# Loading SSM constants as rows, transposing them on TensorE, and moving the first exponentials behind a square root

## The chip, the cores and the metric

One core of a Trainium2 chip runs the whole kernel. The metric is the device time of one execution in microseconds (us), and lower is better. A timed run gives six or so executions; I quote their median and range. A profile is taken of one execution, and its "span" runs from the first to the last instruction; the device time is some 1.8 us longer than the span.

The engines: TensorE (PE) multiplies, VectorE (DVE) and ScalarE (ACT) work on elements, GpSimd (POOL) and SyncE (SP) mostly issue transfers. PSUM is the memory that PE writes; here it is cut into four slots.

## The reference, cut to what matters

```python
xn = layernorm(x)                                    # S=2048 rows, D=576 columns
# state space model with 576 states
dt = exp(log_dt);  Lam_bar = exp(dt * (Lambda_re + 1j*Lambda_im))
B_bar = ((Lam_bar - 1) / Lam)[:, None] * (B_re + 1j*B_im)
h[t] = Lam_bar * h[t-1] + xn[t] @ B_bar.T
ssm = 2 * real(h @ C.T) + xn * Dskip
# gated feed-forward, F=4608
ffn = (sigmoid(xn @ w_gate) * (xn @ w_up)) @ w_down
out = x + ssm + ffn
```

The three vectors `log_dt`, `Lambda_re`, `Lambda_im` have 576 values each. They are needed as per-partition columns: one state per partition, five columns.

## The kernel before

PE does nearly everything that counts: gate/up "groups" of 18 matmuls (two 64-row halves side by side, tile `pgu`), down-projection steps (`pd`), and the SSM's input projections (`pbu`). ACT evacuates each gate/up group from PSUM (sigmoid into `sT`, copy into `uT`), and DVE multiplies the two into `hT`. All other work of DVE and ACT (layernorm of later blocks, residuals, exponentials, angle tables) waits in a background queue. Each evacuation grants it some credit, and it then puts tasks into the instruction streams, in the order in which they were added:

```python
class Background:
    def gap(self): ...            # rest until the next step
    def step(self, us):           # called after each evacuation
        self.now += 1
        self.credit = min(self.credit + us, 5.0)
        while True:
            q = self.head()       # first task whose `ready` holds
            if q is None or q[0][0] > self.credit: return
            cost, fn, _ = q.popleft(); self.credit -= cost; fn()
```

Each engine runs its own stream in order, so a task that is put ahead of an evacuation delays it. The constants are loaded late, one value per partition, by nine POOL-issued transfers, and the exponentials follow much later:

```python
def load_consts():                                    # called after the first 8 groups
    for (dst, src) in ((ldt, A_log_dt), (lre, A_Lambda_re), (lim, A_Lambda_im)):
        nc.gpsimd.dma_start(dst[:, 0:PT], src[0:R0].rearrange("(a p) -> p a", p=P))
        for h0 in (0, H):
            nc.gpsimd.dma_start(dst[h0:h0 + H, PT:NU], src[R0:NS].rearrange("(a b) -> a b", b=1))

def exp_first():
    nc.scalar.activation(dt[:], ldt[:], ACT.Exp)
    nc.vector.tensor_mul(r5[:], dt[:], lre[:])
    nc.scalar.activation(r5[:], r5[:], ACT.Exp)
```

The start, where four PSUM slots hold two gate/up groups and two transpose tiles:

```python
start_groups = [GateUp(0, f, 0) for f in range(2)]
ptrs = [psum.tile([P, NH, P], BF16, name="ptr", tag="ps") for _ in range(2)]
...                                   # block 0: layernorm, PE transposes, first halves
for tt in range(2, TT_B):
    start_copy(tt, slice(0, 5), nc.scalar.copy)
    start_copy(tt, slice(5, NH), nc.vector.tensor_copy)
for g in start_groups:
    g.mms(slice(2 * P, TB))           # second halves of groups 0 and 1
for tt in range(TT_B, 2 * TT_B):
    bg.add(1.05, lambda tt=tt: ln_stats(tt))          # DVE, block 1
bg.gap()
bg.add(0.0, lambda: ln_std(1, 0, TT_B))               # ACT square root
bg.add(0.2, lambda: ln_recip(1, 0, TT_B))
...                                   # normalise, transpose, residuals
bg.gap()
bg.add(1.0, exp_first, ready=...)
bg.gap()
bg.add(1.5, angles_small)             # then ten angle tables on DVE
bg.step(3.2)
for g in start_groups:
    g.evac(); used(g); bg.step(4.5)
```

## Time and profile before

| | us |
|---|---|
| device time, median of 3 | 510.02 (508.99 to 510.29) |
| with three more, median of 6 | 509.67 (508.61 to 510.29) |
| profiled execution: device time, span | 508.32, 506.5 |
| PE busy | 500.9, 99% of the span |

Two rows from the page's costliest groups (line, engine, operation, output and inputs, shapes, count; then busy us and mean ns of one; then the engine's idle time just before them and who ended most of it):

```profile
L495 PE MATMUL pgu<-xT,wgu 64*128 64x512 bf16 (+1 forms) x2628 | 283.7, 373 | 0.0
L569 PE MATMUL pd<-wd,hT 128*128 128x288 bf16 x1152 | 144.8, 286 | 0.4 <-DVE hT L504 0.4
```

The two kinds of matmul wait for others for 0.4 us in all. So in this execution almost nothing can be won by making another engine faster.

### The profile page before, as it was taken

To read this page: it belongs to the slowest core of one execution; us is meant where nothing else is said; L and a number is where in the kernel's file an instruction comes from. 1 tells how busy PE (TensorE), PEld (TensorE's weight loads), DVE (VectorE), ACT (ScalarE), POOL (GpSimd) and SP (SyncE) were. 2 spreads that over 40 slices of the span, in tenths; PEclk is the share of its full clock that TensorE was granted. 3 is DMA by queue.
4 is the path that set the end of the run, shared out by engine and by line. 5 is a ranking of instruction groups with operands and counts; after the bars stand their busy time and mean duration, and the time that the engine had idled before them with its cause. 6 is when DMAs were issued, how large, how long until landed. Compare 5 with 4: busy or idle time off the path is not lost.

```text
span 506.5 us, 10662 instructions
## 1 busy us (share of the span) xinstructions
PE 500.9 (99%) x4536; PEld 290.1 (57%) x4536; DVE 324.1 (64%) x703; ACT 204.9 (40%) x368; POOL 96.9 (19%) x143
## 2 busy tenths in 40 slices
PE   8999999999999999999999999999999999999997
PEld 6444575444477444477754444774444774446775
DVE  6964999886888797868878767786765222221111
ACT  4767623556500756520035655006555005553000
POOL 7138420123100043110001231000431001300000
PEclk9999999999999999999999999999999999999999
DMA  8999895246220099261430652200753201600001
GB/s 211 206 181 163 204 188 98 55 110 141 49 48 25 1 145 199 58 149 37 89 77 11 155 132 55 49 25 1 160 114 79 48 25 39 171 1 4 33 25 36
DMA packets 42959, 45.59 MB, mean 90 GB/s; under 512 B 30496, under 2 KB 34336, under 8 KB 42912
## 3 DMA queue, kind: packets, MB, share of 16 engines
q0 software_dynamic: 12672, 34.23, 31.1%
q1 hardware_dynamic: 29808, 10.33, 10.7%
q8 instruction: 35, 0.57, 0.5%
q10 hardware_dynamic: 432, 0.37, 0.2%
q14 instruction: 12, 0.10, 0.1%
HBM read 34.36 MB, written 2.36 MB: 72 GB/s over the span
## 4 chain that ended last, share of the span: by engine, by line
PE 94%; DVE 3%; ACT 1%; DMA 1%; issue 0%
PE pgu L495 52%; PE pd L569 34%; PE pbu L524 7%; DVE sctab L325 1%; DVE rnd L324 1%; DMA xt<-in_A_x_dram 1%; DVE ang L349 1%; PE ptr L741 0%; DVE hT L504 0%; ACT xT L744 0%; DVE bnst L224 0%; ACT L328 0%; ACT uT L502 0%; ACT L501 0%; ACT sT L501 0%
## 5 line engine op out<-in xcount | busy, mean ns | idle before, releaser
L495 PE MATMUL pgu<-xT,wgu 64*128 64x512 bf16 (+1 forms) x2628 | 283.7, 373 | 0.0
L495 PEld LDWEIGHTS <-wgu 64*128 64x128 bf16 x2628 | 127.6, 94 | 151.1 <-issue 0.5
L569 PE MATMUL pd<-wd,hT 128*128 128x288 bf16 x1152 | 144.8, 286 | 0.4 <-DVE hT L504 0.4
L501 ACT ACTIVATE sT<-pgu 128x512 bf16<-128x512 f32 x144 | 86.4, 600 | 120.4 <-PE pgu L495 110.3
L569 PEld LDWEIGHTS <-hT 128*128 128x128 bf16 x1152 | 112.1, 98 | 31.3 <-DVE hT L504 1.5
L504 DVE TENSOR_TENSOR hT<-sT,uT 128x512 bf16<-128x512 bf16 x144 | 60.7, 423 | 100.3 <-ACT uT L502 100.1
L502 ACT CAST uT<-pgu 128x512 bf16<-128x512 f32 x144 | 83.9, 583 | 0.0
L154 POOL DMA_DIRECT2D wgu<-in_B_w_gate_dram x36 | 27.9, 776 | 227.2 <-PE pgu L495 208.2
L160 POOL DMA_DIRECT2D wd<-in_B_w_down_dram x36 | 26.6, 755 | 100.2 <-PE pd L569 100.2
L530 ACT COPY bure<-pbu 128x512 f32<-128x512 f32 x16 | 9.4, 588 | 87.8 <-PE pbu L524 75.4
L589 DVE TENSOR_TENSOR acc<-acc,pd 128x576 f32<-128x576 f32 x32 | 24.1, 752 | 24.5 <-PE pd L569 24.5
L586 DVE TENSOR_TENSOR ob<-acc,pd 128x576 bf16<-128x576 f32 x15 | 11.3, 754 | 38.0 <-PE pd L569 38.0
L524 PE MATMUL pbu<-xT,bt 64*128 64x512 bf16 x288 | 33.7, 376 | 0.0
L569 PEld LDWEIGHTS <-hst 128*128 128x128 bf16 x288 | 28.2, 98 | 7.1
L154 POOL DMA_DIRECT2D wgu<-in_B_w_up_dram x36 | 26.8, 745 | 2.7 <-DMA wgu<-in_B_w_up_dram 1.9
L569 PE MATMUL pd<-ctre,hst 128*128 128x288 bf16 x128 | 26.5, 286 | 0.0
L569 PE MATMUL pd<-ctim,hst 128*128 128x288 bf16 x128 | 26.5, 286 | 0.0
L439 DVE TENSOR_TENSOR_SCAN gre<-r,g0re,wrim 128x512 bf16<-128x512 f32 x20 | 25.6, 1279 | 0.0
L524 PEld LDWEIGHTS <-bt 64*128 64x128 bf16 x288 | 13.7, 94 | 17.1 <-issue 0.7
L446 DVE TENSOR_TENSOR_SCAN gim<-r,g0im,wrim 128x512 bf16<-128x512 f32 x16 | 20.4, 1275 | 0.0
L224 DVE BATCH_NORM_STATS2 bnst<-xt 128x6 f32<-128x288 bf16 x32 | 12.6, 435 | 2.2 <-DMA xt<-in_A_x_dram 2.2
L501 ACT ACT_TABLE_LOAD x6 | 7.7, 1283 | 15.5 <-PE pgu L495 15.4
(113 smaller groups left out, 280.8 us busy)
## 6 DMA issues: line engine op xcount, KB each, us to landing
wgu<-in_B_w_gate_dram POOLq DMA_DIRECT2D x36, 288.0 KB, 4.4
wgu<-in_B_w_up_dram POOLq DMA_DIRECT2D x36, 288.0 KB, 5.2
wd<-in_B_w_down_dram POOLq DMA_DIRECT2D x36, 288.0 KB, 6.1
out_dram<-ob SPq DMA_DIRECT2D x15, 144.0 KB, 1.8
xt<-in_A_x_dram SPq DMA_DIRECT2D x10, 144.0 KB, 2.8
xt<-in_A_x_dram POOLq DMA_DIRECT2D x4, 144.0 KB, 6.6
bt<-ctre POOLq DMA_DIRECT2D x2, 288.0 KB, 7.2
bt<-ctim POOLq DMA_DIRECT2D x2, 288.0 KB, 8.0
```

Source lines behind the costliest of these rows:

```text
L154: eng.dma_start(w[rows, :, :], src[:, fs].rearrange("(c p) f -> p c f", p=H))
L160: nc.gpsimd.dma_start(wd[:], B_w_down[f0:f0 + FP * P, :].rearrange("(n p) d -> p n d", p=P))
L224: nc.vector.bn_stats(st[:, gi, :], xt[:, gi * DH:(gi + 1) * DH])
L439: nc.vector.tensor_tensor_scan(gre[:], r_bc, w[:, 0, :], g0re[:, col], ALU.mult, ALU.add)
L446: nc.vector.tensor_tensor_scan(gim[:], r_bc, w[:, 1, :], g0im[:, col], ALU.mult, ALU.add)
L495: nc.tensor.matmul(self.ps[:, gi, cols], w[rows, c, fs], xT[self.nb][rows, c, cols], start=c == 0, stop=c == NH - 1)
L501: nc.scalar.activation(sT[:], self.ps[:, 0, :], ACT.Sigmoid)
L502: nc.scalar.copy(uT[:], self.ps[:, 1, :])
L504: nc.vector.tensor_mul(h[:], sT[:], uT[:])
L524: nc.tensor.matmul(out, w, xT[self.nb][rows, c, ts_], start=c == 0, stop=c == NH - 1)
L569: nc.tensor.matmul(out, lhsT, rhs[:, a * DH:(a + 1) * DH], start=i == 0, stop=i == n - 1)
L589: nc.vector.tensor_add(halves(acc[:]), halves(acc[:]), pd[:, :, 0:DH])
```

## The change

Its intent is to get the constants to the chip cheaply and early: three row loads of 64 states per partition instead of nine loads of single values, two small PE transposes in a spot where PE has its operands anyway, and the exponentials next to a square root, so that the long angle tables can start earlier. Apart from that, the last down-projection step is cut 448 + 128 columns rather than 288 + 288, so that less is left to do after the last matmul.

```diff
-    def load_consts(): ...                     # nine POOL loads, see above
+    cvals = consts.tile([P, 3, NU], FP32, name="cvals")
+    ldt, lre, lim = (cvals[:, i, :] for i in range(3))
+    crows = consts.tile([3 * NH, H], BF16, name="crows")
+    for i, src in enumerate((A_log_dt, A_Lambda_re, A_Lambda_im)):
+        nc.sync.dma_start(crows[i * NH:(i + 1) * NH, :], src.rearrange("(a p) -> a p", p=H))
+
+    def consts_transpose(ps):
+        for half in (slice(0, H), slice(H, P)):
+            nc.tensor.transpose(ps[half, 0:3 * NH], crows[:], ident[0:3 * NH, 0:3 * NH])
+
+    def consts_copy(ps):
+        rows = ps[:, 0:3 * NH].rearrange("p (i a) -> p i a", a=NH)
+        nc.vector.tensor_copy(cvals[0:H, :, :], rows[0:H, :, 0:NH:2])
+        nc.vector.tensor_copy(cvals[H:P, :, 0:PT], rows[H:P, :, 1:NH:2])
+        nc.vector.tensor_copy(cvals[H:P, :, PT:NU], rows[H:P, :, NH - 1:NH])
...
     def exp_first():
-        nc.scalar.activation(dt[:], ldt[:], ACT.Exp)
-        nc.vector.tensor_mul(r5[:], dt[:], lre[:])
-        nc.scalar.activation(r5[:], r5[:], ACT.Exp)
+        nc.scalar.activation(dt[:], ldt, ACT.Exp)
+        for a in range(NU):
+            nc.scalar.activation(r5[:, a:a + 1], lre[:, a:a + 1], ACT.Exp, scale=dt[:, a:a + 1])
...                                             # last step of the down projection
-            for a, eng in ((0, nc.sync), (1, nc.scalar)):
-                cs = slice(a * DH, (a + 1) * DH)
+            for eng, cs in ((nc.sync, slice(0, D - P)), (nc.scalar, slice(D - P, D))):
...
-    ptrs = [psum.tile([P, NH, P], BF16, name="ptr", tag="ps") for _ in range(2)]
+    ptrs = [psum.tile([P, NH + 1, P], BF16, name="ptr", tag="ps") for _ in range(2)]
...
-    for g in start_groups:
-        g.mms(slice(2 * P, TB))
+    start_groups[0].mms(slice(2 * P, TB))
+    consts_transpose(ptrs[1][:, NH, :])
+    consts_copy(ptrs[1][:, NH, :])
+    start_groups[1].mms(slice(2 * P, TB))
     for tt in range(TT_B, 2 * TT_B):
         bg.add(1.05, lambda tt=tt: ln_stats(tt))
     bg.gap()
     bg.add(0.0, lambda: ln_std(1, 0, TT_B))
+    bg.add(0.0, exp_first)
...
-    bg.gap()
-    bg.add(1.0, exp_first, ready=lambda: consts_at[0] is not None and consts_at[0] + 4 <= bg.now)
...
-                side_loads.extend([load_consts] + bt_loads)
+                side_loads.extend(bt_loads)
```

The cuts hide renamed operands (`lre[:]` to `lre` and the like), a loop of two loads written out, and the lines of the last step that follow from its new cut.

More of the change, by code (lines that the diff above doesn't have):

```diff
@@ L166 @@
         load_x(tt, nc.sync if tt % 2 == 0 else nc.scalar)
-    for pr in range(2):
-        load_wgu((0, pr), nc.gpsimd, nc.gpsimd)
+    load_wgu((0, 0), nc.gpsimd, nc.gpsimd)
+    load_wgu((0, 1), nc.gpsimd, nc.gpsimd)
     for tt in range(TT_B, 2 * TT_B):
@@ L184 @@
     xn_bufs = [consts.tile([P, NH, 2, H], BF16, name=f"xn{i}") for i in range(XN_BUFS)]
-    lre = consts.tile([P, NU], FP32, name="lre")
-    lim = consts.tile([P, NU], FP32, name="lim")
-    ldt = consts.tile([P, NU], FP32, name="ldt")
-    consts_at = [None]
-    def load_consts():
-        for (dst, src) in ((ldt, A_log_dt), (lre, A_Lambda_re), (lim, A_Lambda_im)):
-            nc.gpsimd.dma_start(dst[:, 0:PT], src[0:R0].rearrange("(a p) -> p a", p=P))
-            for h0 in (0, H):
-                nc.gpsimd.dma_start(dst[h0:h0 + H, PT:NU], src[R0:NS].rearrange("(a b) -> a b", b=1))
-        consts_at[0] = bg.now
+    cvals = consts.tile([P, 3, NU], FP32, name="cvals")
[11 more added lines that the diff above has]
+        nc.vector.tensor_copy(cvals[H:P, :, PT:NU], rows[H:P, :, NH - 1:NH])
     iota = ssmp.tile([P, TB], FP32, name="iota", tag="buim", bufs=2)
@@ L327, in exp_first @@
     def exp_first():
-        nc.scalar.activation(dt[:], ldt[:], ACT.Exp)
-        nc.vector.tensor_mul(r5[:], dt[:], lre[:])
-        nc.scalar.activation(r5[:], r5[:], ACT.Exp)
+        nc.scalar.activation(dt[:], ldt, ACT.Exp)
+        for a in range(NU):
+            nc.scalar.activation(r5[:, a:a + 1], lre[:, a:a + 1], ACT.Exp, scale=dt[:, a:a + 1])
     def angles_small():
-        nc.vector.tensor_mul(thc[:], dt[:], lim[:])
+        nc.vector.tensor_mul(thc[:], dt[:], lim)
         nc.vector.tensor_scalar_mul(thc[:], thc[:], 1.0 / TWO_PI)
@@ L365, in per_state_q @@
         nc.vector.tensor_mul(ni[:], r5[:], sn)
-        nc.vector.tensor_mul(m1[:], lre[:], lre[:])
-        nc.vector.tensor_mul(m2[:], lim[:], lim[:])
+        nc.vector.tensor_mul(m1[:], lre, lre)
+        nc.vector.tensor_mul(m2[:], lim, lim)
         nc.vector.tensor_add(m1[:], m1[:], m2[:])
         nc.vector.reciprocal(m1[:], m1[:])
-        nc.vector.tensor_mul(qre[:], nr[:], lre[:])
-        nc.vector.tensor_mul(m2[:], ni[:], lim[:])
+        nc.vector.tensor_mul(qre[:], nr[:], lre)
+        nc.vector.tensor_mul(m2[:], ni[:], lim)
         nc.vector.tensor_add(qre[:], qre[:], m2[:])
         nc.vector.tensor_mul(qre[:], qre[:], m1[:])
-        nc.vector.tensor_mul(qim[:], ni[:], lre[:])
-        nc.vector.tensor_mul(m2[:], nr[:], lim[:])
+        nc.vector.tensor_mul(qim[:], ni[:], lre)
+        nc.vector.tensor_mul(m2[:], nr[:], lim)
         nc.vector.tensor_sub(qim[:], qim[:], m2[:])
@@ L572, in d_step @@
             ob = lnp.tile([P, D], BF16, name="ob", bufs=2)
-            for a, eng in ((0, nc.sync), (1, nc.scalar)):
-                cs = slice(a * DH, (a + 1) * DH)
-                pd = ps_pair("pd")
+            for eng, cs in ((nc.sync, slice(0, D - P)), (nc.scalar, slice(D - P, D))):
+                pd = ps_pair("pd")[:, 0, 0:cs.stop - cs.start]
                 for i in range(n):
-                    mm(pd[:, 0, 0:DH], i, a)
-                nc.vector.tensor_add(ob[:, cs], acc[:, cs], pd[:, 0, 0:DH])
+                    lhsT, rhs = terms[i]
+                    nc.tensor.matmul(pd, lhsT, rhs[:, cs], start=i == 0, stop=i == n - 1)
+                nc.vector.tensor_add(ob[:, cs], acc[:, cs], pd)
                 eng.dma_start(o[tt * P:(tt + 1) * P, cs], ob[:, cs])
```

## The prediction

> **What bounds the kernel now.** I first read the page's busy times and its chain that ended last.
>
> ```profile
> PE 500.9 (99%) x4536; PEld 290.1 (57%) x4536; DVE 324.1 (64%) x703; ACT 204.9 (40%) x368; POOL 96.9 (19%) x143
> ...
> PE 94%; DVE 3%; ACT 1%; DMA 1%; issue 0%
> ```
>
> The columns are busy us, share of the 506.5 us span and instructions; the second line is the chain's share by engine. TensorE (PE) is the bound. But a busy PE can hide short waits, so I computed the distance from each matmul's start to the next over the whole trace. From 8.48 us (first real matmul) to 502.5 us the spacing is regular: 18 gate/up matmuls, two row halves running side by side, every 1.94 us; 123 ns between the 288-column matmuls of the down projection. Only one spacing stands out: 640 ns instead of 123, in the first down-projection step. The PE timeline shows where:
>
> ```profile
> 37.82 18.73 PE L495 MATMUL pgu<-xT,wgu 64*128 64x512 bf16 x172
> 56.48 2.87 PE L569 MATMUL pd<-wd,hT 128*128 128x288 bf16 x22
> 59.70 6.54 PE L569 MATMUL pd<-wd,hT 128*128 128x288 bf16 x52 [0.35 <-DVE hT L504]
> ```
>
> Columns: start us, duration us, engine, line, operation, tiles, count, and in brackets the idle time before and who ended it. After 22 matmuls (11 of 12 terms) PE waits for the twelfth hT, which VectorE (DVE) made late because it works on the angle tables in between. That wait costs 0.64 - 0.12 = 0.52 us. So the existing kernel has 0.52 us of PE wait to win between start and end, plus whatever lies before 8.48 us and after 502.79 us. Nothing else that gets faster on DVE, ScalarE (ACT), GpSimd (POOL) or a queue can shorten it. The reverse question is where PE has little slack. The timeline of the start answers it:
>
> ```profile
> 11.62 0.42 DVE L744 COPY xT<-ptr 128x512 bf16<-128x512 bf16 x1 [0.17 <-ACT xT L744]
> ...
> 11.96 0.81 DVE L224 BATCH_NORM_STATS2 bnst<-xt 128x6 f32<-128x288 bf16 x2
> ...
> 13.39 0.58 ACT L502 CAST uT<-pgu 128x512 bf16<-128x512 f32 x1
> ...
> 13.99 1.28 ACT L228 ACT_TABLE_LOAD   x1
> ...
> 16.16 0.30 ACT L228 ACTIVATE rstd<-mv,eps_t 128x4 f32<-128x4 f32 x1 [0.89 <-DVE mv L225]
> 16.48 1.28 ACT L501 ACT_TABLE_LOAD   x1
> ...
> 17.77 0.60 ACT L501 ACTIVATE sT<-pgu 128x512 bf16<-128x512 f32 x1
> 18.26 0.58 ACT L502 CAST uT<-pgu 128x512 bf16<-128x512 f32 x1
> ```
>
> ACT evacuates gate/up group 0 (until 13.97), then loads the square-root table and stands waiting for block 1's statistics until 16.16, reloads the sigmoid table and only then evacuates group 1 (done at 18.84). PSUM has four slots: two for the transposes, two for groups 0 and 1. Groups 2 and 3 take the transpose slots, group 4 that of group 0, group 5 that of group 1. The matmul starts in the trace put group 2 at 13.65 and group 5 at 13.65 + 3 x 1.94 = 19.48 us. So the slack of PE against group 1's evacuation is 19.48 - 18.84 = 0.64 us. This is the place to watch.
>
> **What the Trainium skill says.** "ScalarE: Activation LUTs", section What ACT_TABLE_LOAD costs: a table load measures about 1283 ns plus a drain of about 1380 ns. The trace agrees on the load (1283 ns in its groups) but not on a further drain: the load at 16.48 ends at 17.76 and the sigmoid starts at 17.77. I use 1.28. The same section says that each per-partition pointer operand adds about 93 ns to an ACTIVATE and that back-to-back ones overlap by about 93 ns; here a square root with a pointer bias takes 298 ns, the exponential without one 209, and the two square roots at 8.31 us take 0.49 together, so it agrees. "TensorEngine Tiling (Array Packing)", section Key Properties: changing the tiling mode drains the engine; here the step from the last transpose to the next gate/up matmul is 152 ns, against 28 between transposes. "TensorE: Matmul & The Clock Gate", section on the HAM clock gate: after one idle window of about 3.4 us the clock drops to half. This trace shows the clock at 1.0 throughout and no such gap after the start, so it cannot say; it matters below.
>
> **The change part by part.**
>
> *Loads.* Nine POOL-issued loads are removed (about 5.5 us of POOL issue from 35.02 to 40.5 us) and three on the SyncE queue behind x are added; that queue is idle until 17.60. POOL's weight loads move up, but PE waits for none of them: worth 0.
>
> *Two small transposes on PE* between the second halves of groups 0 and 1, at about 12.67 us. 28 ns each and two mode switches; estimate +0.2 us, straight onto the path.
>
> *Three copies on DVE.* In the changed program's order they stand right behind the last xT copy and ahead of block 1's statistics. They can't start before those transposes: 12.67 + 0.2 + 0.26 (the delay from the last transpose's start to ACT's copy: 10.04 to 10.30) = 13.1. Small DVE operations take 0.15 to 0.2 each: about 0.4. The statistics start at 13.5 rather than 11.96: +1.5 us, and so does everything behind them.
>
> *Exponentials behind the square root.* ACT's order now is: square-root table, rstd, exponential table, dt, five one-column exponentials with a pointer scale, sigmoid table, group 1's evacuation. Timed from the rows above: rstd 16.16 + 1.5 = 17.66, done 17.96; table load to 19.26; dt 0.21 to 19.47; 0.06 for the wait on dt, then 4 x 0.2 + 0.29 = 1.09, to 20.62; sigmoid table to 21.92; the two evacuations 0.49 + 0.58, to 22.99; PE goes on 0.05 later, at about 23.05 instead of 19.48. That moves PE by +3.55 us (the 0.2 of the transposes is inside it); as idle time it is about 3.35 us. Of it 0.2 is PE's own, 1.5 comes by DVE's order, 2.4 from the new instructions on ACT, less the slack. Behind it ACT catches up (0.96 us for each group against PE's 1.94), and a saturated PE never wins a shift back.
>
> *What it wins later.* The old exponentials with their two table loads (42.14 to 45.38) leave ACT; PE did not wait there: 0. The angle tables start several groups earlier; in the new DVE order the last angle is followed by six hT without one between, so the 0.52 us wait at 59.06 should go: -0.52.
>
> *The end.* The last step's columns are cut 448 + 128 instead of 288 + 288. PE streams the same 576 columns (warm 128-column matmuls step by 56 ns at 7.14 us), so it ends at the same time. The last DVE addition shrinks: 288 columns take 0.455, 576 take 0.754, so 1.04 ns a column and 0.29 for 128: -0.17. The last output is 256 instead of 576 bytes a row, whose packets took 0.42 us from first to last: perhaps -0.1. Together about -0.25.
>
> Sum: +3.55 - 0.52 - 0.25 = +2.8 us on 510.0: 512.8 us.
>
> **The rivals.** First: the change pays, because ACT's delay is hidden. Then only +0.2 - 0.52 - 0.25 remain, 509.4 us. For it speaks that PE has been slow to notice ACT anywhere else: four slots give up to three groups (5.8 us) of slack. Against it: group 1 is the one group whose slack is down to 0.64 us, and the change puts 3.9 us in front of its evacuation. Second: the stall passes a whole idle window and the clock halves for one window more, which costs about another 1.7 us (half of 3.4): 514.5 us. For it: 3.35 is close to 3.4; against it: the window would have to lie exactly on the gap. Third: block 1's xT becomes the limit, since statistics, normalisation and the queue's transposes are all 1.5 us later. Their last issue ends at 24.93, and the first block-1 group starts at 29.19, or 32.7 with the shift, so there is room: adds 0. Fourth: only DVE's part is smaller than I think (the copies are quick, the transposes come early): the stall would be 2.5 us and the total 512.
>
> **Range and chances.** Runs of the kernel before scatter from 508.99 to 510.29, about 0.65 either way; the stall is uncertain by about 0.6, and the half clock pulls upward with a chance of some 7%. I take 510.9 to 514.6 for 8 in 10, centred at 512.7. Two per cent is 10.2 us, out of reach of every rival: same 0.97, slower 0.02, faster 0.01.
>
> **What would show it.** In the changed profile: PE idle of 3 to 3.5 us near 19.7 us, released by ACT's uT of group 1; rstd of block 1 near 17.7 and an exponential table load right behind it; statistics starting near 13.5; no wait in the first down-projection step; the last addition near 0.29 us. PE going through 19.7 us without a gap would make the prediction wrong, and so would a reading of the clock below 1.0 after it, or new waits of PE between 35 and 60 us where the angle tables move to.

## The result, and the profile after

| | before | after |
|---|---|---|
| median of 6 executions | 509.67 us | 511.37 us |
| range | 508.61 to 510.29 | 510.59 to 512.59 |
| profiled execution: span | 506.5 | 510.7 |
| ratio, 95% interval | | 1.0039 (1.0018 to 1.0060) |

A ratio is the mean time of one kernel's fast runs over that of the other's of the same rounds, so it is not quite the ratio of the medians quoted. An execution more than 1.5% above the fastest of its kernel counts as slow and is left out. By the 2% rule the kernels are the same; in fact the changed one is slower by about 0.4%.

The six executions fall into two clumps: 510.59, 510.67 and 510.76 us at a mean granted clock of 1.0 (the share of its full speed that PE was allowed), and 511.98, 512.57 and 512.59 us at 0.997. The profiled execution is of the second kind. Its page, busy times and chain that ended last:

```profile
PE 503.3 (99%) x4538; PEld 293.2 (57%) x4538; DVE 324.8 (64%) x705; ACT 204.5 (40%) x371; POOL 91.1 (18%) x134
...
PE 97%; ACT 1%; DVE 1%; issue 0%
...
L501 PE MATMUL pgu<-xT,wgu 64*128 64x512 bf16 (+1 forms) x2628 | 285.8, 375 | 3.2 <-ACT uT L508 3.1
```

The last row answers to the first of the two rows shown of before. Two things have changed in it. The idle time before the gate/up matmuls is 3.2 us instead of 0.0, and 3.1 of it was ended by ACT's `uT`. And their busy time rose by 2.1 us for the same 2,628 instructions.

The timeline of the start shows the wait being made (columns: start us, duration us, engine, line, operation; in brackets the idle time before, and who ended it):

```profile
11.91 0.42 DVE L750 COPY xT<-ptr 128x512 bf16<-128x512 bf16 x1 [0.17 <-ACT xT L750]
...
13.05 0.20 PE L196 MATMUL ptr<-ident,crows 27*64 27x27 bf16 x2
...
13.30 0.17 DVE L201 CAST cvals<-ptr 64x15 f32<-64x15 bf16 x1 [0.96 <-PE ptr L196]
...
13.76 0.82 DVE L230 BATCH_NORM_STATS2 bnst<-xt 128x6 f32<-128x288 bf16 x2
...
17.98 0.30 ACT L234 ACTIVATE rstd<-mv,eps_t 128x4 f32<-128x4 f32 x1 [2.41 <-DVE mv L231]
18.29 1.28 ACT L334 ACT_TABLE_LOAD   x1
...
19.58 0.21 ACT L334 ACTIVATE dt<-cvals 128x5 f32<-128x5 f32 x1
19.82 1.04 ACT L336 ACTIVATE r<-cvals,dt 128x1 f32<-128x1 f32 x5
20.86 1.28 ACT L507 ACT_TABLE_LOAD   x1
22.16 0.60 ACT L507 ACTIVATE sT<-pgu 128x512 bf16<-128x512 f32 x1
22.65 0.58 ACT L508 CAST uT<-pgu 128x512 bf16<-128x512 f32 x1
...
23.28 1.00 PE L501 MATMUL pgu<-xT,wgu 64*128 64x512 bf16 x4 [3.11 <-ACT uT L508]
```

DVE is idle for 0.96 us until the transposes give it something to copy; the statistics come behind that; the square root waits 2.41 us for them instead of 0.89; and then the two table loads and six exponentials stand ahead of group 1's evacuation. PE needs that group's slot for group 5 and idles for 3.11 us.

The second thing is in the stretches right behind the wait (columns: stretch, its length, busy us and instructions of PE, PE's weight loads, DVE, ACT and POOL, granted clock, DMA share, GB/s):

```profile
20.00:24.00 4.00, 0.89 (x6) 0.29 (x5) 2.47 (x5) 3.98 (x10) 0.00 (x0) 0.92 0.92 135
24.00:28.00 4.00, 4.00 (x27) 1.86 (x25) 3.86 (x9) 2.57 (x6) 0.00 (x0) 0.65 1.00 186
28.00:32.00 4.00, 4.00 (x40) 2.14 (x38) 3.93 (x9) 2.74 (x6) 0.00 (x0) 1.00 0.98 175
```

Both last stretches show PE busy for the full 4.00 us, but it got through 27 matmuls in the first and 40 in the second. The granted clock was 0.65 in one and 1.00 in the other. The trace's clock record says: half speed from 23.37 us for 3.413 us, and full speed again. A busy PE column alone would have hidden this loss.

Later, the wait in the first down-projection step (59.06 to 59.70 us before) is gone: that step starts at 61.99 us and its matmuls run at their regular distance. Its line, and two from the end:

```profile
61.99 8.26 PE L575 MATMUL pd<-wd,hT 128*128 128x288 bf16 x66
...
507.77 0.29 DVE L584 TENSOR_TENSOR ob<-acc,pd 128x128 bf16<-128x128 f32 x1 [0.55 <-PE pd L583]
508.09 0.36 ACTq L585 DMA_DIRECT2D out_dram<-ob  x1
```

Before, the last addition was of 288 columns and took 0.46 us from 502.79 us on.

### The profile page after: what moved, and what is told of

It is laid out like the page before. It is cut to its first block, busy times and chain, and to the rows that moved or that the text cites. A ratio compares the mean times of both kernels' runs of the same rounds, so it can differ in the third digit from the quotient of the medians.

```text
span 510.7 us, 10663 instructions
## 1 busy us (share of the span) xinstructions
PE 503.3 (99%) x4538; PEld 293.2 (57%) x4538; DVE 324.8 (64%) x705; ACT 204.5 (40%) x371; POOL 91.1 (18%) x134
## 4 chain that ended last, share of the span: by engine, by line
PE 97%; ACT 1%; DVE 1%; issue 0%
PE pgu L501 54%; PE pd L575 34%; PE pbu L530 7%; PE pd L583 1%; PE pgu L739 1%; DVE bnst L230 1%; PE ptr L747 0%; ACT xT L750 0%; ACT L507 0%; ACT L334 0%; ACT r L336 0%; DVE mv L231 0%; ACT sT L507 0%; ACT uT L508 0%; ACT rstd L234 0%
## 5 line engine op out<-in xcount | busy, mean ns | idle before, releaser
L501 PEld LDWEIGHTS <-wgu 64*128 64x128 bf16 x2628 | 130.9, 94 | 152.6 <-issue 5.8
L575 PE MATMUL pd<-wd,hT 128*128 128x288 bf16 x1128 | 141.4, 286 | 0.0
L575 PEld LDWEIGHTS <-hT 128*128 128x128 bf16 x1128 | 109.9, 98 | 30.1 <-DVE hT L510 1.3
L575 PEld LDWEIGHTS <-hst 128*128 128x128 bf16 x270 | 26.4, 98 | 6.7
L575 PE MATMUL pd<-ctre,hst 128*128 128x288 bf16 x120 | 24.5, 286 | 0.0
L575 PE MATMUL pd<-ctim,hst 128*128 128x288 bf16 x120 | 24.5, 286 | 0.0
L432 DVE TENSOR_TENSOR tq<-T,buim 128x512 bf16<-128x512 bf16 x20 | 13.7, 685 | 0.0
```

The source lines that it names most:

```text
L501: nc.tensor.matmul(self.ps[:, gi, cols], w[rows, c, fs], xT[self.nb][rows, c, cols], start=c == 0, stop=c == NH - 1)
L575: nc.tensor.matmul(out, lhsT, rhs[:, a * DH:(a + 1) * DH], start=i == 0, stop=i == n - 1)
```

## The experiments

Twelve runs in three batches of four. The first and third ran on chip 11 and share most of their executions of the kernel before; the second ran on chip 0 and has its own. All results were correct, and one execution of one run was slow and is left out where it is told. "Gap" below means PE's idle time near 20 us in the profile, as its timeline states it.

**First batch: both kernels again, the suspected parts undone, and the end alone.** The theory: the gap is the loss, made by two orders (copies ahead of the statistics on DVE, exponentials ahead of group 1's evacuation on ACT), and whether the clock falls on top of it is a matter of where the gap lies in a fixed grid of windows. Rivals: the kernels' times differ by chance of the runs, or by the constants' loads.

*The kernel before, unchanged.*

> The kernel before, unedited, to learn what its 508.6 to 510.3 us scatter is made of. Theory (the scatter is in the start, where x arrives): a profile of another execution has the same spacing of matmuls after the first one, with the same 0.52 us wait in the first down-projection step, and only the first real matmul moves from 8.48 us. Rival (the scattered 2-byte loads of the constants sometimes land late, ScalarE waits for them near 42 us and TensorE behind it): the wait in the first down-projection step or a gap before it is larger than 0.52 us. Ratio 1.000, clock 1.000 in every run for both.

Measured: 509.42 us (508.96 to 509.59), ratio 0.9987 (0.9968 to 1.0007), span 507.7 us at a clock of 0.999. So its time repeats. But this profiled execution (509.47 us) is an ordinary one, which the first (508.32 us) was not, and it shows more waits of PE than the first:

```profile
21.75 0.46 DVE L264 TENSOR_TENSOR tmpxd<-xn,dskip_rows 128x576 bf16<-128x576 bf16 x1 [1.24 <-DMA dskip_rows<-in_A_Dskip_dram]
...
29.92 3.41 PE L495 MATMUL pgu<-xT,wgu 64*128 64x512 bf16 x30 [0.30 <-ACT uT L502]
...
60.88 2.38 PE L569 MATMUL pd<-wd,hT 128*128 128x288 bf16 x18 [0.79 <-DVE hT L504]
```

DVE waited 1.24 us for the skip weights' load, and its later work ran late. (The larger wait in the down-projection step was the sign of my rival, but not by the loads that I had suspected.) From start to start of the matmuls, that cost 0.47 us at 29.92 us, and 0.95 us instead of 0.52 in the first down-projection step. The first real matmul started at 8.74 instead of 8.48 us. Together 0.26 + 0.47 + 0.43 = 1.16 us, which is the difference of the two spans (507.7 - 506.5 = 1.2). The first profile of the kernel before was a lucky execution, and I had based the sum on it.

One of the 21 executions of the kernel before that were run beside the batches took 512.53 us at a clock of 0.995. No profile was taken of it, so the clock can fall without the change too, though rarely.

*The changed kernel, unchanged.*

> The changed kernel, unedited. Theory: two kinds of executions, 510.6 to 510.8 us with the clock at 1.000 and 512.0 to 512.6 us with it at 0.997, about 1.8 us apart, nothing between; the gap near 20 us is 3.1 us of idle in both. Rival (half clock is a property of the run, not of the gap's place in the windows): the gap differs between the two kinds by more than 0.3 us. Ratio 1.002 to 1.006.

Measured: 512.95 us (512.71 to 513.61), ratio 1.0060 (1.0042 to 1.0079); all six executions at a clock of 0.997 or below. The gap is 3.11 us again, and the clock is halved behind it again:

```profile
23.68 6.61 PE L501 MATMUL pgu<-xT,wgu 64*128 64x512 bf16 x44 [3.11 <-ACT uT L508]
```

Six in six is not the rare accident that I had put at 7%. I had expected two kinds of executions here, and only one came.

*Copies on ACT behind group 0's evacuation, exponentials back behind the residuals (`late_act`).* Both suspected orders are undone, while the row loads, the transposes and the new end stay.

```diff
-        nc.vector.tensor_copy(cvals[...], rows[...])      # three times
+        nc.scalar.copy(cvals[...], rows[...])
...
-    consts_copy(ptrs[1][:, NH, :])                        # right behind the transposes
+    bg.add(0.0, lambda: consts_copy(ptrs[1][:, NH, :]))   # behind the ln_stats tasks
     bg.gap()
     bg.add(0.0, lambda: ln_std(1, 0, TT_B))
-    bg.add(0.0, exp_first)
...                                                        # behind the residuals
+    bg.add(1.0, exp_first)
+    bg.gap()
     bg.add(1.5, angles_small)
```

> The changed kernel with the exponentials back behind the residuals and the three small copies moved from VectorE to ScalarE, behind group 0's evacuation. Theory (the gap is group 1's evacuation, delayed by those two things alone): no gap near 20 us, group 5 starts 1.94 us after group 4; no wait in the first down-projection step; clock 1.000 in every run; 2.8 to 3.1 us less than the changed kernel's fast-clock runs, so about 507.7 us, ratio to the kernel before 0.995 to 0.998. Rival (the gap comes with the transposes on TensorE or the new loads, not with ScalarE): the gap stays at 2 us or more and the ratio at 1.002 or above.

Measured: 507.61 us (507.46 to 507.98), ratio 0.9955 (0.9937 to 0.9973), span 505.6 us. This beats both kernels: 5.34 us below the changed kernel's median of the same batch (512.95). Its ACT timeline:

```profile
13.85 0.17 ACT L201 CAST cvals<-ptr 64x15 f32<-64x15 bf16 x1
...
16.15 0.30 ACT L234 ACTIVATE rstd<-mv,eps_t 128x4 f32<-128x4 f32 x1 [0.59 <-DVE mv L231]
16.47 1.28 ACT L507 ACT_TABLE_LOAD   x1
17.76 0.60 ACT L507 ACTIVATE sT<-pgu 128x512 bf16<-128x512 f32 x1
18.26 0.58 ACT L508 CAST uT<-pgu 128x512 bf16<-128x512 f32 x1
```

The three copies fill time that ACT had spent waiting for the statistics: the square root starts at 16.15 us, as in the kernel before (16.16), and group 1 is evacuated at the old time. There is no gap at 20 us and no fall of the clock. PE waits once, 0.25 us at 33.5 us, behind the moved exponentials.

*The new end alone, on the kernel before (`tail_only`).*

```diff
-            for a, eng in ((0, nc.sync), (1, nc.scalar)):
-                cs = slice(a * DH, (a + 1) * DH)
+            for eng, cs in ((nc.sync, slice(0, D - P)), (nc.scalar, slice(D - P, D))):
```

> The kernel before with the last step's cut of 448 and 128 columns alone. Theory (read from the two profiles: last addition 0.17 us shorter, from its end to the end of the span 0.63 us shorter): 0.5 to 0.8 us less, ratio 0.9984 to 0.9990. As predicted: 0.25 us less, ratio 0.9995. Rival (the tail is the end of other work): 1.000.

Measured: 509.64 us (508.35 to 509.96, and one slow execution of 521.0 left out), ratio 0.9988 (0.9966 to 1.0009): not resolved. The profile decides more than the time. From the end of the last addition to the end of the span it takes 3.35 us, against 3.27 in both profiles of the kernel before and 2.62 and 2.60 in those of the changed kernel. So the new cut does not shorten that stretch; something else in the change does. I had put all of it down to the cut, and that was wrong.

**Second batch: one order at a time, and the cut the other way round.**

*Only the exponentials back (`exp_late`): the last part of the diff of `late_act`.*

> The changed kernel with only the exponentials moved back behind the residuals; the copies stay on VectorE. Theory: block 1's square root is still 1.5 us late (near 18.0 us), but the sigmoid table follows it at once, so group 1's evacuation ends 2.3 us earlier than in the changed kernel and the gap near 20 us shrinks from 3.1 us to 0.5 to 0.9 us; clock 1.000; 0.4 to 0.9 us more than the run with both moved (507.6), so 508.0 to 508.5. Rival (the copies before the statistics are the larger part): the gap stays above 1.5 us.

Measured: 509.03 us (508.65 to 509.28), ratio 0.9997 (0.9984 to 1.0011). The gap shrinks from 3.11 to 0.54 us. The time is worse than I expected, because there is a second wait that I had not foreseen:

```profile
20.92 13.77 PE L501 MATMUL pgu<-xT,wgu 64*128 64x512 bf16 x126 [0.54 <-ACT uT L508]
35.27 2.98 PE L501 MATMUL pgu<-xT,wgu 64*128 64x512 bf16 x26 [0.58 <-ACT uT L508]
```

In this kernel the exponentials and their two table loads occupy ACT from 30.27 to 34.14 us, while ACT has not yet made up for its lateness at the start. Here ACT's 3.9 us do reach PE.

*Only the copies moved to ACT (`copies_act`): the first two parts of the diff of `late_act`.*

> The changed kernel with only the copies moved to ScalarE; the exponentials stay behind the square root. Theory: the square root is back near 16.2 us, the exponentials and their table put 2.5 us ahead of group 1's evacuation, and the gap is 1.4 to 1.9 us; too short for the clock to fall, so clock 1.000 and 1.4 to 2.0 us more than the run with both moved (507.6), 509.0 to 509.6. Rival (any gap of over 1 us lets the clock fall): clock 0.997 and about 511.

Measured: 509.40 us (509.00 to 510.03), ratio 1.0007 (0.9995 to 1.0020). The gap is 1.59 us, 1.52 less than in the changed kernel; the clock stays at 0.999 or above:

```profile
22.46 7.73 PE L501 MATMUL pgu<-xT,wgu 64*128 64x512 bf16 x70 [1.59 <-ACT uT L508]
```

*`late_act` with the old cut of 288 + 288 (`late_oldtail`), and `late_act` with the exponentials two steps later (`late_gap`).*

```diff
+    for _ in range(3):                     # late_gap only: three rests for one
+        bg.gap()
     bg.add(1.0, exp_first)
```

> The kernel with both moved and the old halves of 288 columns in the last step. Theory (from the traces, the new cut ends 0.6 to 0.8 us earlier): 508.2 to 508.4, which is 0.6 to 0.8 more than with the new cut. As predicted: 0.25 us more, 507.9. Rival: no difference, 507.6.

> The kernel with both moved and the exponentials two steps later, when ScalarE has caught up. Theory: the 0.25 us wait of TensorE near 33 us goes and nothing new comes, 0.2 to 0.3 us less: 507.3 to 507.5. Rival (the angle tables now reach into the first down-projection step again): the wait there comes back, 0.3 us or more over 507.6.

Measured: `late_oldtail` 508.07 us (507.68 to 508.34), ratio 0.9981 (0.9968 to 0.9993); `late_gap` 507.69 us (507.37 to 508.00), ratio 0.9973 (0.9961 to 0.9986). The old cut costs about 508.07 - 507.69 = 0.38 us, less than the 0.6 to 0.8 that I expected of it and nearer to the 0.25 of the prediction. The intervals overlap, and part of it may belong to the later exponentials. With the old cut, the stretch from the last addition's end to the end of the span is 2.72 us, nearly as short as in the changed kernel (2.62) and far from 3.27. So most of the short end comes with what these kernels share, the moved constant loads and the transposes; that it is the loads is my inference. In the profile of `late_gap` PE has no wait left between 14 us and the end; but whether the later exponentials save the 0.25 us of `late_act` can't be told from times on two chips. `late_oldtail` has its exponentials where `late_act` has them, and its profile doesn't show that wait either, so the wait doesn't come in every execution.

**Third batch: the order of evacuation and square root, and how long a gap the clock tolerates.**

*One more rest, so that group 1's evacuation comes ahead of the square root and the exponentials: with the copies on ACT (`evac_first`), and as the only edit of the changed kernel (`evac_first_dve`).*

```diff
     for tt in range(TT_B, 2 * TT_B):
         bg.add(1.05, lambda tt=tt: ln_stats(tt))
     bg.gap()
+    bg.gap()
     bg.add(0.0, lambda: ln_std(1, 0, TT_B))
     bg.add(0.0, exp_first)
```

> The changed kernel with the copies on ScalarE and group 1's evacuation ahead of the square root; the exponentials stay right behind the square root. Theory (what counts is which evacuation stands behind the table loads, and group 2's is not wanted before 21.4 us): ScalarE is done with group 2 near 21.5 us, so the gap is 0 to 0.3 us, clock 1.000, and as no table load comes in later, 507.2 to 507.7 us, ratio 0.995 to 0.998. Rival (the table loads and exponentials cost TensorE time wherever they stand here): a gap of 1.5 us or more before group 6, 509 or more.

> The changed kernel with group 1's evacuation ahead of the square root and nothing else (the copies stay on VectorE before the statistics). Theory: group 2 is evacuated where group 1 was (near 23.2 us), group 6 wants its slot at about 21.9, so a gap of 1.2 to 1.5 us, clock 1.000, 508.7 to 509.2 us. Rival (only group 1's place matters): no gap, 507.5.

Measured: `evac_first` 507.92 us (507.70 to 508.55), ratio 0.9962 (0.9941 to 0.9983); `evac_first_dve` 509.02 us (508.63 to 509.31), ratio 0.9980 (0.9961 to 0.9999). The wait moves by one group, as it must, since group 2 is now the one behind the exponentials. It is 0.17 us long in the first and 1.17 us in the second:

```profile
23.41 6.87 PE L501 MATMUL pgu<-xT,wgu 64*128 64x512 bf16 x62 [1.17 <-ACT uT L508]
```

`evac_first` is a little slower than I expected (507.2 to 507.7). One line more in the changed kernel takes 510.76 - 509.02 = 1.74 us off it (the changed kernel of the same batch is `after3`, below), with its copies and exponentials in place. That puts it just clear of the kernel before. PE reaches the slot of group 2 one group later, and ACT has that much more time.

*A gap on purpose (`gap_mid`): `copies_act` with every one-column exponential done twice, the second time into a scratch tile.*

```diff
         for a in range(NU):
             nc.scalar.activation(r5[:, a:a + 1], lre[:, a:a + 1], ACT.Exp, scale=dt[:, a:a + 1])
+            nc.scalar.activation(extra[:, a:a + 1], lre[:, a:a + 1], ACT.Exp, scale=dt[:, a:a + 1])
```

> The changed kernel with the copies on ScalarE and every one-column exponential done twice, the second into a tile that nothing reads: a gap between the 1.6 us idle of the run with the copies moved and the 3.1 us of the changed kernel. Theory of additive work: 5 x 0.2 = 1.0 us more idle, 2.6 us, and 1.0 us over the run with the copies moved if the clock stays: 510.4. For the clock two readings: if a window of 3.4 us must be idle whole it never falls; if a window that is idle for most of its length is enough, it falls in some executions (0.997) and these take 1.7 us more, about 512.

> The changed kernel again on another chip, for the clock: two readings as in the run with the middle gap. If the fall depends on how the gap of 3.1 us lies in the free-running windows, some executions fall (0.997, about 512.8) and some don't (1.000, about 510.8), and in the profile the window before a fall contains the gap almost whole; if it depends on the chip, all six go one way.

Measured: `gap_mid` 510.53 us, ratio 1.0015 (0.9990 to 1.0041); the changed kernel for the third time (`after3`) 510.76 us, ratio 1.0026 (1.0002 to 1.0050). The gap of `gap_mid` is 2.62 us in its profile, 1.03 more than the 1.59 of `copies_act`: five more exponentials at 0.2 us. Two of its six executions, 511.93 and 511.94 us, had a clock of 0.997; the others, 510.01 to 511.02 us, had 1.0. Of the six of `after3`, two (512.36 and 512.97 us) had 0.997, and four (510.43 to 510.90 us) had 1.0. The profiled one was among the latter:

```profile
22.86 7.52 PE L501 MATMUL pgu<-xT,wgu 64*128 64x512 bf16 x68 [3.11 <-ACT uT L508]
```

The gap is the very same 3.11 us, with another outcome. The chip doesn't decide it: contrary to the plan, `after3` ran on chip 11 again, where `after2` had fallen six times in six. From the clock records I worked out the windows. In the first profile of the changed kernel the clock is full for 17.067 us, half for 3.413 and full for 484.693, which are 5, 1 and 142 times 3.413 us. So the grid is fixed by the clock's first rise. In that profile (rise at 6.30 us) one window runs from 19.95 to 23.37 us and holds the entire gap; PE was busy for 0.30 us of it, 9%, and the clock was halved for the next window. In `after2` a window holds 2.89 us of the gap (15% busy), and the clock fell too. In `after3` the gap is cut by a window's edge into 1.58 and 1.53 us, and it did not fall. Nor did it in the profiled execution of `gap_mid` (1.45 and 1.17), in that of `copies_act` (1.59 in one window, 53% busy) or of `evac_first_dve`. The reading by windows fits every profile, but I did not set the gap's place in the grid, only observed it.

## Why the prediction was right or wrong

The prediction said 512.7 us (510.9 to 514.6), and the median was 511.37 us. The class and the range hold, and so does the mechanism of the wait. But one of the signs that the prediction named as making it wrong came true: a reading of the clock below 1.0 behind the gap. Below, `after3` serves for comparison with the first profile of before, since both ran at a full clock throughout.

| stretch of the span | before | after3 | difference | predicted |
|---|---|---|---|---|
| start to first real matmul | 8.48 | 8.34 | -0.14 | 0 |
| from there to the start of the last addition | 494.31 | 497.32 | +3.01 | +3.55 - 0.52 = +3.03 |
| last addition | 0.46 | 0.29 | -0.17 | -0.17 |
| from there to the end | 3.27 | about 2.6 | about -0.7 | -0.1 |
| span | 506.5 | 508.5 | +2.0 | +2.8 |

The second row is from 8.48 to 502.79 us before and from 8.34 to 505.66 us in `after3`. From start to start of the matmuls, the wait puts group 5 back by 3.28 us (the 3.11 of idle time begin only at the modelled end of the last matmul), and 3.28 + 0.24 for the transposes - 0.52 = 3.00.

- **The two PE transposes**: predicted +0.2 us; from the first real matmul to group 2 it took 13.65 - 8.48 = 5.17 us before and 14.18 - 8.77 = 5.41 after, so +0.24. Right.
- **The copies delay the statistics by 1.5 us**: right. The statistics start at 13.76 us and the square root at 17.98, of which 0.29 is the later start of this execution. Shown by experiment: moving only the copies takes 3.11 - 1.59 = 1.52 us off the gap.
- **The exponentials delay group 1's evacuation by 2.4 us**: right, with 3.11 - 0.54 = 2.57 us in the experiment that moves only them. (The prediction's own timeline gives 22.99 - 18.84 - 1.5 = 2.65; its 2.4 is a slip that its sum does not use.) The two parts add up to 4.09 us of idle time and the gap is 3.11. From start to start it closes better: group 5 is put back by 3.28 us with both, by 1.76 with the exponentials alone and by 0.70 with the copies alone, so the slack is 3.28 - 1.76 - 0.70 = 0.82 us. In `late_act`, with both moved, there is no gap, and group 1 is evacuated 0.87 us before PE wants its slot; PE follows an evacuation after 0.05, which leaves 0.82. The prediction's 0.64 plus the 0.24 by which the transposes hold PE itself back is 0.88.
- **The first rival, that ACT's delay is hidden**, falls. **The third, block 1's xT**, falls too: no wait for it in any profile. **The fourth, a smaller part of DVE**, falls with the 1.52 us.
- **The wait in the first down-projection step goes**: right in all profiles of the changed kernel.
- **The constants' loads are "worth 0"**: wrong in size and in place. No PE wait hung on them, but the end of the span is 0.55 to 0.68 us shorter in every kernel with the moved loads (2.59 to 2.72 us in eleven profiles) than in the first profile of before (3.27, 3.27 and 3.35 us in the three with the old loads). In the trace's epilogue, SP checks four semaphores of 0.06 us each after the last landing instead of seven, since the last output's semaphore stands later in its list: 0.19 us. POOL's clearing of the semaphores follows 0.3 us sooner; why, I leave open. The remaining 0.15 us is the last output, which lands 1.51 to 1.53 us after the last addition instead of 1.67. Of this the prediction had said "perhaps -0.1". It goes with the new cut where the loads are moved (`late_oldtail` has 1.64), but not with the old loads (`tail_only` has 1.78), so the cut's share is not settled.
- **The half clock as a rival with a chance of "some 7%"**: the term that failed most. Going by the mean clock of 0.997 or less, it happened in 3, 6 and 2 of six executions, so in 11 of 18. I had argued that the window would have to lie exactly on the gap, as for a window that must be wholly idle. In the runs a window that was 15% busy was followed by the fall, and even with the shorter gap of `gap_mid` two of six executions have the lower clock (neither was profiled). Its cost was guessed well: predicted 1.7 us; from the first real matmul to the last addition, the first profile took 499.00 us (8.77 to 507.77) and `after3` 497.32, so 1.68.
- **The sum's base**: an error that the prediction did not see. The sum was worked out on a profiled execution of 508.32 us, whose waits amount to 0.52 us, and then added to the median of 510.02 us. Ordinary executions of the kernel before have some 1.2 us more of waits and late starts, as the profile of `before2` shows, and in no profile of the changed kernel does PE have them. That is why the executions at full clock are at 510.4 to 510.9 us: they are the 508.32 of the profile plus some 2.3, not the median plus 2.8.

So two errors of opposite sign are in the number: the base was too high by about 1.7 us against the profiled execution, and the half clock, which costs as much, was left out of the centre. A third, of some 0.6 us, is the end. Where the clock falls the time is 512.0 to 513.6 us, close to the 512.7 predicted; where it does not, it is below the range or at its edge. The median of the first six lies between the clumps. The range held for a reason that was partly luck.

The same account explains the better kernel. From the first real matmul (8.47 us) to the last addition (502.75 us) `late_act` takes 494.28 us, as long as the lucky execution of before (494.31) and 0.94 less than the ordinary one (8.74 to 503.96, 495.22). Those 0.94 are the two waits of `before2`, 0.47 + 0.95, less the transposes' 0.24 and its own wait of 0.25. The remainder of its 2.1 us of span (507.7 to 505.6) is the start (0.27, which is scatter: in the three profiles of the changed kernel the first real matmul starts at 8.34, 8.77 and 9.17 us), the smaller addition (0.17) and the shorter end (0.66).

What stays open: whether every ordinary execution of before has the waits seen in `before2` (one profile of such an execution exists, and the times fit it; that of `tail_only`, an execution of 508.35 us, has none of them beyond the 0.5 us in the first down-projection step); why the clearing of the semaphores ends sooner; what the cut alone is worth; where between 15% and 53% of busy time in a window the fall begins; and which of `late_act`, `late_gap` and `evac_first` is best, for their intervals overlap and they ran on two chips.

## What to carry to other kernels

When one engine is the bound, look for the place where it has the least slack and ask of every added instruction in which engine's stream it stands and what stands behind it: the same copies cost 1.5 us on DVE ahead of the statistics, and nothing on ACT, which was waiting for these statistics. Here a wait of PE of 3.11 us had a second price in 11 of 18 executions, 1.7 us paid afterwards at half clock; so price it as likely, and look at the granted clock rather than at busy time. Check that the profiled execution's own time is typical before adding a sum worked out on it to a median.

## What the Trainium skill lacked or had wrong

- "TensorE: Matmul & The Clock Gate", section on the HAM clock gate: it says that the clock drops after an idle window of about 3.4 us, in a free-running window of 3413 ns. The length agrees (half clock for 3.413 us, on a fixed grid). It does not say how idle a window must be: here a window with PE busy for 9%, and one with 15%, was followed by the half clock; one with 53% was not. A gap of 3.11 us, shorter than the window, was followed by it in 11 of 18 executions. A limit between 15% and 53% was not measured.
- "ScalarE: Activation LUTs", section What ACT_TABLE_LOAD costs: the load itself agrees (1.28 us). The further drain of about 1380 ns does not show: the load starts at 20.86 us, where the exponentials end, it ends at 22.14, and the sigmoid starts at 22.16; a switch of tables costs 1.28 to 1.3 us here. The same section's pointer operand and overlap agree with five one-column exponentials in 1.04 us.
- "TensorEngine Tiling (Array Packing)", section Key Properties: it says that a change of the tiling mode drains the engine and gives no duration. Two small transposes between 64-row matmuls, with a switch on either side, cost 0.24 us together here.
- "Runtime: NRT & Kernel Launch" has a table of stages behind a kernel (a barrier, a reset of semaphores), but no page that I found tells how the end of a program depends on the transfers that it uses: 3.27 to 3.35 us from the last addition to the end of the span with the nine POOL loads, 2.59 to 2.72 us with the three row loads in their place.
